# Batched attention with memory and a two-layer gated network on one core: first-layer operands of all batches split from the attention's sums, without x in DRAM

## The chip, the cores and the metric

The kernel runs on one core of a Trainium2 chip. The metric is the device time of one execution in microseconds; the time given is the median of the runs. A profiled execution has a time of its own, which is given beside its span (first to last instruction).

## The reference

Two parts run one after the other. The attention: 4 batches, 8 heads, 576 positions, 64 wide; causal softmax attention, mixed by a gate per head with a retrieval from a memory matrix. The result x, 2304 tokens by 512, goes through a two-layer network with a sigmoid gate.

```python
scores = q @ k.T / sqrt(D)                       # causal mask, softmax -> a
local = a @ v
q_p = where(q > 0, q, exp(q) - 1) + 1
mem_out = (q_p @ M_prev) / (q_p @ z_prev + 1e-6)
x = g * mem_out + (1 - g) * local                # g = sigmoid(beta), one per head
h = x @ w_in                                     # 512 -> 2048
out = (h * sigmoid(1.702 * h)) @ w_out           # 2048 -> 512
```

## The kernel before

**Precision.** The network's weights arrive as 64-bit floats. The kernel rebuilds them as 32-bit floats (`conv_unit`, `conv_pair`) and splits each operand into a high part and a low part (`xh`, `xl` for x; `wi` and `wo` for the weights); a product is three matmuls: high x high, low weight x high, high weight x low.

**Attention.** Work goes by pairs of heads: 16 pairs, four to a batch (`pairs`, index p, c is the pair within the batch). `plan_attend` lays the steps of a pair over numbered slots from `K0[p]` on: scores, softmax on VectorE and ScalarE, scaling on GpSimd, transposes, and the products with v and the memory into one PSUM tile `po` (`pv_both`; the pool `ps_o` holds one). A pair has two such sums: queries 256 to 575 (ch 1, 320 wide) and, one slot later, queries 0 to 255 (ch 0). For batch 0 the second is done up front by `first_queries`. `xboth` (L616) copies a sum to `xf` in SBUF, on VectorE for ch 1 and on ScalarE for ch 0, and keeps the copy's name in `values["po"]`; the next group of matmuls that writes `po` waits for it. Score matmuls may be put into the same group, and then wait too.

**From x to the first layer.** The first layer goes by chunks of queries, eight in all: 256 and 320 for batch 0, 288 and 288 for the others. `xstore` (L643) stores each pair's `xf` into the DRAM tile `xd`. When a batch's four pairs are done, `plan_x` (L704) loads a chunk into `xl` and `split_x` (L241) makes `xh` (ScalarE) and the low part in place (GpSimd). `xopen` (L634) does this early for the first three pairs of a batch's first chunk, if the chunk two before is done; the fourth pair then comes straight from `xf` (`xdirect`, L622). The pool `mop` holds two chunks of `xh` and `xl`. All these DMAs, the loads of later pairs and the stores of first-layer results go through the one queue of SyncE, in order.

**First layer.** `first_moe` (L724) makes for each chunk 16 blocks of 12 matmuls into `pm`; `gate` copies `pm` to `hk` (three buffers, ScalarE and VectorE in turn) and stores `hk` to the DRAM tiles `gd`.

**The order.** `step` runs a slot's planned pieces by priority, adding up a cost for each matmul (`mm`), and then fills the slot with first-layer matmuls up to the cost in `PACE`, which depends on the slot's number: L42. If the first layer has no chunk to work on, the slot stays short. The tile framework orders each engine's instructions by these priorities and its own estimate of what is ready.

**After the attention.** The attention's pools on the right side of SBUF are closed and the space is used again by `w2a` (the first five pieces of converted w_out), `opa`, `g11a` and `stg`; a tile there waits only for the tiles that lay under it. While TensorE finishes the first layer, `conv_pair` converts w_out: ScalarE scales, VectorE puts bits together and forms sums and low parts. Then the second layer runs: 84 products of 12 matmuls 384 wide, into `acc` (L935). Its fourth product is the first to use the last two pieces of w_out.

## Time and profile before

| | us |
|---|---|
| median of 3 runs | 641.17 (640.54 to 646.22) |
| profiled execution, its own time | 648.07 |
| its span | 646.3 |
| TensorE busy in the span | 602.6 (93%) |
| VectorE busy | 414.3 (64%) |
| ScalarE busy | 363.0 (56%) |
| GpSimd busy | 183.7 (28%) |
| mean granted TensorE clock | 0.985 |

PE is TensorE's matmuls, PEld its weight loads, DVE VectorE, ACT ScalarE, POOL GpSimd, SP SyncE (SPq its queue). "Released by" is what ended a wait. Matmul ends are modelled, so a busy TensorE need not be one at its peak. PEclk is the granted clock as a share of 2.4 GHz.

### The profile page before, as it was taken

The numbers are of one execution on the slowest core, as the hardware profiler recorded it, in microseconds if no ns is written. First come the engines' busy times: TensorE is split into PE (matmuls) and PEld (weight loads), VectorE is DVE, ScalarE is ACT, GpSimd is POOL, SyncE is SP. The second block draws the span as 40 slices with busy tenths as digits, with TensorE's granted clock in tenths as the row PEclk, the third lists the DMA queues.
The fourth block names the chain that finished last, engine by engine and source line by source line (L and its number), as shares of the span: only waits on it lengthen the run. The fifth ranks groups of instructions, "written<-read, shape, count | busy, mean of one in ns | idle before, by whom it ended". The sixth has DMA issues, their size and how long they took to land.

```text
span 646.3 us, 11501 instructions
## 1 busy us (share of the span) xinstructions
PE 602.6 (93%) x4000; PEld 522.7 (81%) x4000; DVE 414.3 (64%) x1015; ACT 363.0 (56%) x836; POOL 183.7 (28%) x253
## 2 busy tenths in 40 slices
PE   3698998999979999989999999899989999999997
PEld 2458765688657787778888889899989999999996
DVE  3998866654665445544455437889496579458944
ACT  4776575544564468354554335665876764776451
POOL 3556644532456433343544112310000000000000
PEclk9988999999999999999999999899999999999999
DMA  8848642323444155243342115775745630671002
GB/s 248 297 148 261 186 158 88 129 70 129 138 134 138 52 177 167 73 153 96 123 153 83 49 66 186 231 238 173 238 145 171 186 133 15 206 212 57 25 2 73
DMA packets 59370, 90.61 MB, mean 140 GB/s; under 512 B 5680, under 2 KB 48176, under 8 KB 59312
## 3 DMA queue, kind: packets, MB, share of 16 engines
q1 hardware_dynamic: 57008, 81.49, 40.1%
q0 software_dynamic: 2304, 8.39, 4.2%
q8 instruction: 31, 0.51, 0.3%
q14 instruction: 27, 0.22, 0.1%
HBM read 63.02 MB, written 26.84 MB: 139 GB/s over the span
## 4 chain that ended last, share of the span: by engine, by line
PE 66%; DMA 12%; ACT 9%; DVE 7%; issue 3%; SPq 1%; POOL 1%; DVEq 0%; ACTq 0%; POOLq 0%
PE acc L935 23%; PE pm L125 22%; PE po L125 7%; PE pt L131 7%; PE ps L125 7%; DMA gd<-hk 3%; DMA xl<-xd 3%; DMA xd<-xf 2%; DMA g<-gd 2%; ACT a L485 2%; DMA fq<-in_vq_dram 1%; DVE g L144 1%; ACT hk L136 1%; DMA qr<-in_vq_dram 1%; DVE ps L479 1%
## 5 line engine op out<-in xcount | busy, mean ns | idle before, releaser
L125 PE MATMUL pm<-xh,wi 128*128 128x288 f32 (+2 forms) x1024 | 219.4, 307 | 11.3 <-ACT hk L136 5.9
L125 PEld LDWEIGHTS pm<-xh,wi 128*128 128x128 f32 x1024 | 168.5, 194 | 14.9 <-ACT hk L136 7.0
L935 PE MATMUL acc<-oh,wo 128*128 128x384 f32 x672 | 158.3, 337 | 0.9 <-ACT oh L136 0.7
L125 PE MATMUL pm<-xl,wi 128*128 128x288 f32 (+2 forms) x512 | 154.3, 303 | 0.0
L935 PEld LDWEIGHTS acc<-oh,wo 128*128 128x128 f32 x672 | 120.0, 188 | 2.7 <-ACT oh L136 2.7
L144 DVE TENSOR_TENSOR ol<-g,oh 128x768 fp32r<-128x768 f32 x84 | 79.2, 955 | 49.0 <-ACT oh L136 44.4
L479 DVE CUSTOM_DVE_ANT_0 ps<-ps,mask 128x256 f32<-128x256 f32 (+4 forms) x144 | 67.5, 506 | 61.6 <-PE ps L125 54.8
L488 POOL TENSOR_SCALAR a<-a,sm,g 128x512 f32<-128x512 f32 (+3 forms) x112 | 71.6, 651 | 116.4 <-DVE sm L538 100.0
L935 PE MATMUL acc<-ol,wo 128*128 128x384 f32 x336 | 99.7, 339 | 2.7 <-DVE ol L144 2.6
L125 PEld LDWEIGHTS pm<-xl,wi 128*128 128x128 f32 x512 | 98.6, 193 | 1.1 <-DVE wr L216 1.1
L485 ACT ACTIVATE a<-ps,nm 128x256 f32<-128x256 f32 (+2 forms) x112 | 59.9, 542 | 63.9 <-DVE nm L479 63.1
L136 ACT ACTIVATE oh<-g 128x768 fp32r<-128x768 f32 x84 | 70.2, 840 | 42.3 <-PE acc L935 40.9
L125 PE MATMUL ps<-kqf 128*128 128x288 f32 (+4 forms) x288 | 67.9, 480 | 4.6 <-ACT at L485 2.3
L935 PEld LDWEIGHTS acc<-ol,wo 128*128 128x128 f32 x336 | 61.5, 188 | 5.3 <-DVE ol L144 5.3
L136 ACT ACTIVATE hk<-pm 128x288 f32<-128x288 f32 (+2 forms) x85 | 34.1, 410 | 38.2 <-PE pm L125 26.8
L131 PE MATMUL pt<-ident,a 128*128 128x128 f32 x296 | 53.2, 274 | 0.0
L898 ACT ACTIVATE g<-g 128x768 f32<-128x768 f32 x48 | 40.3, 844 | 20.3 <-DMA g<-gd 17.8
L125 PEld LDWEIGHTS po<-e,vr 128*64 128x64 f32 x416 | 29.9, 137 | 20.1
L131 PE MATMUL pt<-ident,at 128*128 128x128 f32 x160 | 41.4, 285 | 4.9 <-ACT a L485 3.5
L125 PE MATMUL po<-e,vr 128*64 128x320 f32 (+3 forms) x416 | 45.4, 359 | 0.0
L144 DVE TENSOR_TENSOR g<-g,g 128x768 f32<-128x768 f32 x48 | 44.1, 953 | 1.2 <-ACT g L898 1.1
L125 PEld LDWEIGHTS ps<-kqf 64*128 64x128 f32 (+1 forms) x288 | 30.1, 189 | 17.8 <-issue 7.4
(127 smaller groups left out, 751.5 us busy)
## 6 DMA issues: line engine op xcount, KB each, us to landing
g<-gd SPq DMA_DIRECT2D x48, 384.0 KB, 3.9
gd<-hk SPq DMA_DIRECT2D x96, 144.0 KB, 2.0
wraw<-in_w_out_dram POOLq DMA_DIRECT2D x16, 512.0 KB, 4.8
wraw<-in_w_in_dram SPq DMA_DIRECT2D x16, 512.0 KB, 4.8
kqf<-in_kq_dram SPq DMA_DIRECT2D x12, 608.0 KB, 6.6
vr<-in_vq_dram SPq DMA_DIRECT2D x16, 320.0 KB, 6.0
qr<-in_vq_dram SPq DMA_DIRECT2D x12, 320.0 KB, 3.2
xd<-xf SPq DMA_DIRECT2D x10, 288.0 KB, 6.4
```

Source lines behind the costliest of these rows:

```text
L125: x = nc.tensor.matmul(out, l, r, start=start, stop=stop)
L131: nc.tensor.transpose(out, in_, idn)
L136: return nc.scalar.activation(out=dst, in_=src, func=AF.Copy, **kw)
L144: (nc.vector if eng == "V" else nc.gpsimd).tensor_tensor(out=dst, in0=a, in1=b, op=op)
L479: nc.vector.tensor_tensor_reduce(out=ps, in0=ps, in1=mk, op0=ALU.add, op1=ALU.min, scale=-0.125, scalar=1e38 if j == 0 else nm[:, j - 1:j] ...
L485: return nc.scalar.activation(out=a, in_=ps, func=AF.Exp, scale=-1.0, bias=nm, accum_out=sm)
L488: (nc.vector if eng == "V" else nc.gpsimd).tensor_scalar(out=a, in0=a, scalar1=r, scalar2=gcol, op0=ALU.mult, op1=ALU.mult)
L898: nc.scalar.activation(out=t, in_=t, func=AF.Gelu_apprx_sigmoid)
L935: nc.tensor.matmul(acc[b, j][:, :QN], W[2 * p + kk][:, WPART[i], sp, 128 * j:128 * j + 128], mv[:, kk], start=first and p + kk == 0 and sp ...
```

## The change

Every sum of the attention is split straight from PSUM into `xh` (ScalarE) and `xl` (VectorE) by the new `split_sum`; `values["po"]` names the subtract. The copies to `xf`, the DRAM tiles `xd`, their stores and loads, and `split_x`, `split_direct`, `xdirect`, `xopen`, `xstore` and `plan_x` are gone. The operands of two batches are held: those of odd batches in `mop`, those of even ones in a new pool `mox`, the first on the right side. Chunks are 256 and 320 wide for every batch, and a chunk can be used from the slot after its last sum. `PACE` is 2.2 below slot 60 and 2.8 after it.

```diff
@@ -35,11 +35,10 @@
 def tile_attention_memory_moe(ctx, tc, kq, vq, mem, zz, beta, w_in, w_out, out):
     nc = tc.nc
     CH = 288
-    NCH = S // CH
     MB = 1
     KEEP = 1
     STEP = 7
-    PACE = ((20, 2.2), (60, 2.2), (9999, 2.7))
+    PACE = ((60, 2.2), (9999, 2.8))
     LATE = 4
     W0 = 6
     CONV = [-7, -6, -5, -3, -1, 1, 3, 5, 7, 9]
...
@@ -58,6 +57,7 @@
     fst = pool(first, "fst", side="left")
     ps_m = pool(left, "ps_m", 2, space=PSUM, side="left")
     dr = pool(ctx, "dr", space=bass.MemoryType.DRAM)
+    mox = pool(attn, "mox", 2, side="right")
     ldp = pool(attn, "ldp", side="right")
     att = pool(attn, "att", side="right")
     wkp = pool(attn, "wkp", side="right")
...
@@ -66,7 +66,6 @@
     ps_x = pool(attn, "ps_x", 1, space=PSUM, side="right")
     ps_o = pool(attn, "ps_o", 1, space=PSUM, side="right")
 
-    xd = [dr.tile([128, NK, S], F32, name=f"xd{b}") for b in range(B)]
     gd = [dr.tile([2, 128, NT], F32, name=f"gd{k}") for k in range(NB // 2)]
 
     moe_ps = [(ps_m, "pm")]
...
@@ -227,30 +226,24 @@
             at(slot + k, prio, fn)
 
 
-    chunks = [(b, 0, 256) for b in range(MB)] + [(b, 256, 320) for b in range(MB)]
-    chunks += [(b, CH * ch, CH) for b in range(MB, B) for ch in range(NCH)]
+
+
+    chunks = [(b, a, n) for b in range(B) for a, n in ((0, 256), (256, 320))]
     XW = max(n for _, _, n in chunks)
     xq = {}
     xplan = {}
 
     def new_x(n):
-        xl = mop.tile([128, NK, XW], F32R, name="xl")
-        xq[n] = [None, xl]
-        return xl
-
-    def split_x(n, upto=NK):
-        w, xl = chunks[n][2], xq[n][1]
-        xh = xq[n][0] = mop.tile([128, NK, XW], F32R, name="xh")
-        for c in range(upto):
-            copy("A", xh[:, c, :w], f32(xl[:, c, :w]))
-            sub("P", xl[:, c, :w], f32(xl[:, c, :w]), xh[:, c, :w])
-
-    def split_direct(n, c, src):
+        assert n < 4 or n - 4 in done, n
+        p = mop if chunks[n][0] % 2 else mox
+        xq[n] = [p.tile([128, NK, XW], F32R, name=x) for x in ("xh", "xl")]
+
+    def split_sum(n, c, src):
         w, (xh, xl) = chunks[n][2], xq[n]
         copy("A", xh[:, c, :w], src)
-        sub("V", xl[:, c, :w], src, xh[:, c, :w])
-
-    direct, done = set(), set()
+        return tt("V", xl[:, c, :w], src, f32(xh[:, c, :w]), ALU.subtract)
+
+    done = set()
 
     def first_queries(b):
         K, fsm = [], []
...
@@ -339,7 +332,7 @@
                     nc.tensor.transpose(pt[:, o:o + 128], q[:, c, t], ident)
             copy("A", qt[:, 2 * k:2 * k + 2].rearrange("p c q -> p (c q)"), pt)
 
-        def values(c, xl):
+        def values(c):
             po = (ps_o if c % 2 == 0 else ps_m).tile([128, 512], F32, name="pm" if c % 2 else "po")
             rr = [slice(64 * h, 64 * h + 64) for h in range(2)]
             for k, (l, o, mv) in enumerate((
...
@@ -348,13 +341,11 @@
                     (v[:, c, 1], 128, lambda h: fa[c][:, 512 + 128 * h:640 + 128 * h]))):
                 for h in range(2):
                     nc.tensor.matmul(po[rr[h], o:256], l[:, rr[h]], mv(h), start=k == 0, stop=k == 2)
-            copy("A", xq[b][0][:, c, :256], po[:, :256])
-            sub("V", xl[:, c, :256], po[:, :256], xq[b][0][:, c, :256])
+            split_sum(0, c, po[:, :256])
 
         if b == 0:
             gates()
-        xl = new_x(b)
-        xq[b][0] = mop.tile([128, NK, XW], F32R, name="xh")
+        new_x(b)
         score(0)
         phi()
         score(1)
...
@@ -614,40 +604,12 @@
                     mm(po[r, x:y], l[:, r], mv, first and k == 0, last and k == len(ops) - 1)
 
         def xboth(ch):
-            q0, n = (0, 256) if ch == 0 else (256, 320)
-            if ch:
-                P["xf"] = wkp.tile([128, S], F32, name="xf")
-            values["po"] = copy("AV"[ch], P["xf"][:, q0:q0 + n], U["po", ch][:, :n]).ins.name
-
-        def xdirect():
-            n = 2 * b + 1 if rest else 2 * b
-            if rest and c == 0:
-                direct.add(n)
+            n = 2 * b + ch
+            if n not in xq:
                 new_x(n)
-                xq[n][0] = mop.tile([128, NK, XW], F32R, name="xh")
-            if n in direct and (rest or c == NP - 1):
-                a, w = chunks[n][1:]
-                split_direct(n, c, P["xf"][:, a:a + w])
-                if c == NP - 1:
-                    xplan[n] = state["slot"] + 1
-
-        def xopen():
-            n = 2 * b
-            if n in direct or n - 2 not in done:
-                return
-            direct.add(n)
-            a, w = chunks[n][1:]
-            nc.sync.dma_start(f32(new_x(n)[:, :NP - 1, :w]), xd[b][:, :NP - 1, a:a + w])
-            at(state["slot"] + 2, 45, lambda: split_x(n, NP - 1))
-
-        def xstore():
-            if not rest:
-                a = CH if c == NP - 1 and 2 * b in direct else 0
-                nc.sync.dma_start(xd[b][:, c, a:], P["xf"][:, a:])
-            del prep[p]
-            raws.pop(p)
+            values["po"] = split_sum(n, c, U["po", ch][:, :chunks[n][2]]).ins.name
             if c == NP - 1:
-                xready[b] = state["slot"]
+                xplan[n] = state["slot"] + 1
 
         at(k0, 10, s_tail)
         at(k0 + 1, 10, max_tail)
...
@@ -694,22 +656,7 @@
                 at(k + 1, 12, lambda js=js: hand_on(js, pv_both, [U["ev", hh, jj] for hh in range(2) for jj in js]))
                 at(k + 1, 30, flush)
                 at(k + 1, 32, lambda ch=int(j > 0): xboth(ch))
-        if c == NP - 1 and not rest:
-            for j in range(k0 + 7, k0 + 11):
-                at(j, 5, xopen)
-        at(k + 2, 33, xdirect)
-        at(k + 2, 60, xstore)
-
-
-    def plan_x(n, slot):
-        b, a, w = chunks[n]
-
-        def load():
-            nc.sync.dma_start(f32(new_x(n)[:, :, :w]), xd[b][:, :, a:a + w])
-
-        at(slot + 1, 5, load)
-        at(slot + 2, 45, lambda: split_x(n))
-        return slot + 3
+
 
     def gate(ps, n, blk):
         b, a0, w = chunks[n]
...
@@ -724,13 +671,6 @@
     def first_moe():
         after = 0
         for n, (b, _, w) in enumerate(chunks):
-            if n not in xplan:
-                while b not in xready:
-                    yield 1
-                if n not in xplan:
-                    xplan[n] = plan_x(n, state["slot"])
-            if n >= 2 * MB and n % 2 == 0:
-                xplan[n + 1] = plan_x(n + 1, state["slot"] + (n not in direct))
             for blk in range(NB):
                 while blk not in wb or n not in xplan or state["slot"] < xplan[n]:
                     yield 1
```

## Rows read from the trace of the kernel before

**Rows 1.** The page: engines (busy us, share, instructions) and the chain that ended last, by engine and line.

```profile
PE 602.6 (93%) x4000; PEld 522.7 (81%) x4000; DVE 414.3 (64%) x1015; ACT 363.0 (56%) x836; POOL 183.7 (28%) x253
...
PE acc L935 23%; PE pm L125 22%; PE po L125 7%; PE pt L131 7%; PE ps L125 7%; DMA gd<-hk 3%; DMA xl<-xd 3%; DMA xd<-xf 2%; DMA g<-gd 2%; ACT a L485 2%; DMA fq<-in_vq_dram 1%; DVE g L144 1%; ACT hk L136 1%; DMA qr<-in_vq_dram 1%; DVE ps L479 1%
```

**Rows 2.** Busy time by stretches: length; PE, PEld, DVE, ACT, POOL; clock; DMA share; GB/s.

```profile
184.00:193.00 9.00, 5.55 (x35) 3.47 (x34) 5.34 (x22) 5.99 (x20) 4.01 (x6) 1.00 0.66 222
...
193.00:213.00 20.00, 16.89 (x110) 12.44 (x111) 9.32 (x35) 10.75 (x34) 13.62 (x18) 0.91 0.37 116
...
276.00:289.00 13.00, 10.52 (x75) 9.13 (x74) 5.33 (x19) 6.78 (x25) 4.98 (x9) 0.99 0.50 159
...
288.00:293.00 5.00, 4.71 (x25) 4.70 (x26) 0.32 (x2) 2.70 (x8) 3.19 (x5) 0.66 0.25 87
...
414.00:419.00 5.00, 4.44 (x22) 4.44 (x23) 5.00 (x11) 2.71 (x7) 2.02 (x3) 0.66 0.82 233
...
293.00:388.00 95.00, 95.00 (x732) 79.44 (x732) 46.22 (x162) 41.68 (x128) 31.96 (x43) 1.00 0.31 95
...
388.00:459.00 71.00, 68.02 (x505) 67.25 (x500) 58.38 (x105) 44.82 (x93) 14.16 (x20) 0.98 0.65 203
```

**Rows 3.** Timeline of TensorE: start, length, line, tile, count; in brackets idle before, releaser.

```profile
288.29 0.56 PE L125 MATMUL pm<-xh,wi 128*128 128x288 f32 x2 [2.44 <-ACT hk L136]
...
414.56 0.55 PE L125 MATMUL pm<-xh,wi 128*128 128x288 f32 x2 [2.01 <-ACT hk L136]
```

**Rows 4.** Timeline of SyncE's queue, the same columns, issue of DMAs.

```profile
276.37 0.33 SPq L646 DMA_DIRECT2D xd<-xf  x1
...
282.92 0.38 SPq L640 DMA_DIRECT2D xl<-xd  x1
...
283.39 11.73 SPq L720 DMA_DIRECT2D gd<-hk  x6
...
403.40 0.53 SPq L708 DMA_DIRECT2D xl<-xd  x1
```

**Rows 5.** Timeline of ScalarE, the two splits of loaded x.

```profile
286.83 1.11 ACT L136 ACTIVATE xh<-xl 128x288 fp32r<-128x288 f32 x3 [6.17 <-DMA xl<-xd]
...
410.36 1.45 ACT L136 ACTIVATE xh<-xl 128x288 fp32r<-128x288 f32 x4 [3.15 <-DMA xl<-xd]
```

**Rows 6.** Groups by line and shape: busy us, mean ns; last row one tile's view (min/median/max).

```profile
L139 DVE COPY xf<-po 128x320 f32<-128x320 f32 x16 | 7.8, 491 | 6.5 <-PE po L125 6.5
...
L136 ACT ACTIVATE xf<-po 128x256 f32<-128x256 f32 x12 | 4.5, 376 | 1.0 <-PE po L125 1.0
...
L136 ACT ACTIVATE xh<-xl 128x288 fp32r<-128x288 f32 x22 | 8.1, 432 | 16.0 <-DMA xl<-xd 16.0
...
L144 POOL TENSOR_TENSOR xl<-xl,xh 128x288 fp32r<-128x288 f32 x22 | 18.5, 869 | 21.9 <-ACT xh L136 21.9
...
L136 ACT ACTIVATE xh<-xf 128x320 fp32r<-128x320 f32 x4 | 1.8, 457 | 1.1 <-DVE xf L139 1.1
...
L144 DVE TENSOR_TENSOR xl<-xf,xh 128x320 fp32r<-128x320 f32 x4 | 2.2, 545 | 2.3 <-ACT xh L136 2.3
...
L144 DVE TENSOR_TENSOR xl<-po,xh x2: 415/418/420, 31.5 to 36.3; 128x256 fp32r<-128x256 f32 x2
```

**Rows 7.** Timelines around `po`: first a filled stretch, then one without fill.

```profile
366.43 2.22 PE L125 MATMUL po<-e,vr 128*64 128x320 f32 x20
...
371.00 0.92 PE L125 MATMUL ps<-kqf 64*128 64x256 f32 x8
...
180.41 0.49 DVE L139 COPY xf<-po 128x320 f32<-128x320 f32 x1 [0.48 <-PE po L125]
...
181.05 0.92 PE L125 MATMUL ps<-kqf 64*128 64x256 f32 x8
```

**Rows 8.** Timeline of VectorE, the last piece of converted w_out.

```profile
459.55 1.23 DVE L144 TENSOR_TENSOR wo<-st,wo 128x1024 fp32r<-128x1024 f32 x1 [2.76 <-ACT wo L136]
```

**Rows 9.** Waits of ScalarE: us in total, times, longest.

```profile
ACT hk L136 <- DMA gd<-hk: 7.7, 6, 2.3
```

More of the change, by code (lines that the diff above doesn't have):

```diff
@@ L366, in first_queries @@
         qtr(1)
[L367 removed]
+        values(0)
         score(3)
         norm(2)
[L370 removed]
+        values(1)
         norm(3)
[L372 to L373 removed]
+        values(2)
+        values(3)
     pairs = [(b, c) for b in range(B) for c in range(NP)]
```

7 lines of the change are left out of this document (1 added, 6 removed).

## The prediction

> **What bounds the kernel now.** I read the page's engine table and its chain first. TensorE is busy 602.6 of 646.3 us, so 43.7 us of idle time is all there is to win besides clock; on the chain that ended last, DMA holds 12%, with the load of x (xl<-xd) 3% and its store (xd<-xf) 2% [rows 1]. So the second question is where TensorE stands idle. The table by stretches answers it [rows 2]: from 293 to 388 us TensorE has no idle time at all, but it idles 9.00-5.55=3.45 us in 184 to 193, 20.00-16.89=3.11 us in 193 to 213 and 13.00-10.52=2.48 us in 276 to 289. Each of these stands where a batch's x has just been summed and first-layer work on it is about to begin. The timeline of TensorE names the two longest stops after that, 2.44 us at 288.29 and 2.01 us at 414.56, both released by ScalarE's copy `hk` [rows 3]; and after each the granted clock is 0.66 over 5 us [rows 2], so about 3.4 of the 5 us run at the 1.2 GHz level and the rest at 2.4 GHz: 5.00x(1-0.66)=1.7 us of work lost each time. In 193 to 213 the clock is 0.91: 20.00x0.09=1.8 us.
>
> Why would TensorE wait for an `hk` copy? SyncE's timeline and ScalarE's show it [rows 4, 5]. At 276.37 SyncE issues the store of batch 2's last sums; the load of the same data behind it may go only when that store has landed, and goes at 282.92; six `hk` stores queue behind it. ScalarE has `xh<-xl` next in its own order and stands 6.17 us, till 286.83, for the load. Behind that stands `hk`, behind `hk` the PSUM bank that TensorE needs. At 403.40 it is the same with the last chunk: its load waits for chunk 5's buffer, ScalarE stands 3.15 us and goes on at 410.36. So a store, a load and two in-order queues, and not TensorE, end the wait at batch boundaries.
>
> **The change part by part.** The sum starts from the profiled execution: 646.3 us span and 1.8 us around it, 648.07 us. The median of the three runs is 641.17 us; I subtract the same number of microseconds from it. Their scatter (640.54 to 646.22) makes about 1% what can be told from no change.
>
> *x no longer goes through DRAM.* The stores of 12 pairs, the loads of 6 chunks, their waits and the 22 + 22 splits from `xl` (ScalarE 432 ns, GpSimd 869 ns) go [rows 6]. At 184 to 213 the idle time is 6.56 us; from about 184.5, when the sum of pair 7 is split, first-layer matmuls can fill it, and I leave 1.5 us to the start of the stretch: -5.0, and -1.8 for the clock. At 276 to 289: -2.48 and -1.7. At 414: -2.01 and -1.7. Together -14.7 us. Bounds: -16.2 if nothing stays idle, and -8.5 if the idle time of the last two places remains with one of the clock's dips, from another cause (14.7-2.5-2.0-1.7).
>
> *The splits move onto the PSUM sum.* Per whole pair, before: one VectorE copy (491 ns) and one ScalarE copy (376 ns) out of PSUM, then the splits elsewhere. After: ScalarE `xh` and VectorE `xl` for both halves, about 457+376 ns and 545+418 ns by the nearest rows [rows 6]. VectorE's share rises by 0.47 us a pair; it is busy 46.22 of 95 us in 293 to 388 [rows 2], so that is hidden. What is not plainly hidden is the bank `po`, of which there is one: `values["po"]` now names the VectorE subtract, which comes after ScalarE's copy, and the next group (8 score matmuls and the 12 of the second half) stands behind it. In a filled stretch the first half ends at 368.65 and the group begins at 371.00, with first-layer matmuls between: 2.35 us of cover against 0.46+0.55+ about 0.2 of handing over =1.2 us: 0. Without fill, the copy takes 180.41 to 180.90 and the group starts at 181.05 [rows 7]: there TensorE is 0.5 us late, two such pairs: +1.0. Bounds: 0, and +4 if ScalarE's exponentials delay each of 12 pairs so that TensorE stops 0.33 us.
>
> *On the queues.* SyncE loses those 18 issues and the waits in them; the `hk` stores, and the loads of later pairs, stand behind nothing of x. GpSimd loses 22x0.87=19 us and ScalarE the 16.0 us that it stood for loads [rows 6], none of it TensorE's work: 0.
>
> *Chunks of 256 and 320 for 288 and 288.* The same 192 matmuls and columns a chunk pair: 0. Twelve matmuls of 256 columns end 1/9 sooner, so `hk` copies come faster; ScalarE stood 7.7 us for `hk` stores in the whole run [rows 9]. Only batch 3's first half runs without attention between: 0 to +2, I take 0, since those waits cost TensorE little already.
>
> *PACE 2.8 from slot 60 on (2.7 before).* It moves work and adds none: from slot 67, where batch 1 is summed, to 132 66 slots x 0.1=6.6 us of first-layer matmuls run before the attention's end instead of after. The fill must not run dry: by the planner's own costs a whole pair has some 12.1 us of attention, so 8 slots leave 8x2.8-12.1=10.3 us; four pairs use 41 of the 51 us that a batch gives (192x(256+320)/2400 plus 384x0.013). It doesn't.
>
> *What this uncovers: the conversion of w_out.* It runs after the attention, 388 to 459, where VectorE is already busy 58.38 of 71 us; its last piece starts at 459.55 [rows 2, 8] and is needed by the fourth product of the second layer, some 6 us after that layer begins (3 products of (646.3-459)/84=2.2 us). Before, TensorE is busy 68.02 us here, 1.7 of them lost to the clock, and idle 3. After, 66.3 us less 6.6 us moved: about 60 us, while the conversion needs at least its 58 us, and its first two weights now wait for the pool `mox` under them, till chunk 5 is done (403.40 before, 15 us into this stretch [rows 4]; about 8 us into it now). Lower bound 0, upper bound +7 (the conversion as late as before, 72 us from the attention's end, against 60+6): I take +2, nearer the row of VectorE's work than that of its present end, because ScalarE's standing for x (3.15 us [rows 5]) held the conversion up too.
>
> *Room.* `mox` adds 4x5 KB a partition on the right and drops `xf`; no instruction follows: 0.
>
> Sum: -14.7+1.0+0+0+2.0=-11.7 us: 636.4 us for a profiled execution, **629.5 us** against the median.
>
> From the store's issue at 276.37 to the end of ScalarE's wait for the load the rows show 10.5 us, 6.5 of them before the load may go [rows 4, 5]. The Trainium skill (DMA: Bandwidth & Descriptors, Anatomy of one DMA) gives a transfer a fixed cost of about 2 us, most of it the receipt of the write, and lets the rest grow with the bytes. The trace does not agree in this stage; by the skill's figure, an estimate, the two transfers would take some 5 us, the boundary at 276 would have cost nothing, and the sum would be -7.5 us, 633.7 us.
>
> **The rivals.**
> 1. *The conversion becomes the bound.* For it: VectorE's 82% there, and the wait for `mox`. Against: 6 us of slack at the fourth product. At its upper bound, +7, with a clock dip of 1.7: -14.7+1+7+1.7=-5.0, 636.2 us.
> 2. *The stalls only move.* If the filling matmuls are used up before the next batch is summed, the stretch of 184 to 193 comes back before batches 2 and 3: 2x(3.45+1.8)=10.5 us given back, 640.0 us. Against it stands the reserve of 10 of 51 us; for it that the planner's costs are not times.
> 3. *The bank `po` is held too long: slower.* ScalarE then VectorE empty the one bank one after the other, and ScalarE may be in the exponentials. It costs nothing until the subtract ends 2.35 us after the first half's last matmul; each microsecond beyond costs 12 us over 12 pairs. To be over 1% slower it must end (11.7+6.4)/12=1.5 us later still; at 4 us, 12x1.65=19.8 us, 649.3 us. Against: in 293 to 388 ScalarE is busy 41.68 of 95 us. The Trainium skill (VectorE: DVE Perf Modes, Rules for kernel authors) says to copy a matmul's output to SBUF first where several operations follow, which is what the change stops doing. By the rows the subtract itself isn't slower for it: 418 ns for 256 columns from PSUM, 545 ns for 320 from SBUF.
> 4. *The boundary at 276 costs less outside a profile.* The profiled execution is 648.07-641.17=6.9 us longer than the median; if the waits of [rows 4] are part of that, its 2.5+1.7 us are not there to be won: 641.17-(11.7-4.2)=633.7 us. Against: the 6.9 us may lie anywhere.
>
> **How the numbers follow.** Forecast 0.52, rival 1 0.17, rival 2 0.13, rival 3 0.10, rival 4 0.08. The likeliest case alone reaches from 625 (nothing idle left, 0 for po and conversion: -16.2) to 635 (-8.5 and +2). The range of 624 to 642 takes in rivals 1, 2 and 4; beyond it I leave rival 3 and some of rival 2 above (0.14) and 0.06 below. Faster by over 1% (under 634.8): 0.9 of the forecast, 0.35 of rival 1, 0.1 of rival 2, 0.6 of rival 4: 0.59. Slower by over 1% (over 647.6): rival 3 and a little of rival 2, 0.12. Within 1%: 0.29.
>
> **What would show it.** No xd rows and no `xh<-xl` wait on DMA in ScalarE's list; TensorE full from the first matmul of chunk 2 to the end of the attention, and clock 1.00 at the places that answer to 193, 288 and 414 (step 1). First-layer matmuls between any two pairs after batch 1 (step PACE; their lack is rival 2). Less than 2.35 us from the end of the first half to the subtract's end (po; TensorE idle at the score group, released by VectorE, is rival 3). The second layer beginning about 60 us after the last attention product, with at most 2 us of idle time in its first products for `wo` (conversion; more is rival 1). The prediction is wrong at its root if the three places are quiet and the time is still above 636: then TensorE's idle time was not what set the end.

## The result: slower by 1.25%

| us | before | after |
|---|---|---|
| median of four runs | 643.47 (640.54 to 646.22) | 653.08 (650.54 to 655.16) |
| ratio, 95% interval | | 1.0125 (1.0086 to 1.0163) |
| profiled execution, its span | 646.3 | 653.1 |
| attention's last product (`po`) begins | 388.4 | 388.0 |
| first layer's last matmul | 458.4 | 449.6 |
| last piece of w_out (`wo`) begins on VectorE | 459.6 | 466.6 |
| second layer, first matmul to end of span | 187.8 | 203.3 |

629.5 us and a range of 624 to 642 had been forecast. The table shows where to look: the first layer ends 8.8 us sooner, as meant, and the second layer takes 15.5 us longer. -8.8+15.5 is, to rounding, the 6.8 us between the spans. The medians differ by 9.6 us: the profiled execution of the kernel before was 4.6 us longer than its median and that of the changed one 2.1 us, so 2.5 us of the difference are in no trace.

The page of the changed kernel, engines and chain (by engine, then by line), beside [rows 1]: TensorE's busy time is the same. On the chain that ended last the loads and stores of x are gone, and VectorE stands at 11% (7% before).

```profile
PE 603.1 (92%) x4000; PEld 524.9 (80%) x4000; DVE 417.1 (64%) x1024; ACT 355.2 (54%) x817; POOL 164.0 (25%) x231
...
PE 64%; DVE 11%; DMA 10%; ACT 9%; issue 4%; POOL 1%; SPq 1%; DVEq 0%; ACTq 0%; POOLq 0%
PE pm L124 26%; PE acc L875 14%; PE po L124 8%; PE ps L124 8%; PE pt L130 7%; DMA g<-gd 7%; DVE ol L143 3%; ACT oh L135 2%; ACT g L838 2%; DVE g L143 1%; DMA gd<-hk 1%; DVE ps L469 1%; ACT a L475 1%; ACT at L475 1%; DMA fq<-in_vq_dram 1%
```

Busy time by stretches of the changed kernel, in the columns and mostly the stretches of [rows 2]:

```profile
184.00:193.00 9.00, 8.30 (x60) 5.79 (x58) 7.26 (x29) 6.26 (x21) 6.41 (x9) 1.00 0.45 158
193.00:213.00 20.00, 18.76 (x143) 14.13 (x142) 13.32 (x50) 12.68 (x39) 9.92 (x13) 1.00 0.29 99
276.00:289.00 13.00, 13.00 (x94) 12.02 (x93) 5.72 (x21) 6.30 (x21) 4.29 (x7) 1.00 0.35 128
288.00:293.00 5.00, 5.00 (x39) 3.22 (x37) 2.52 (x8) 1.62 (x5) 0.08 (x1) 1.00 0.09 33
414.00:419.00 5.00, 5.00 (x44) 5.00 (x44) 3.88 (x7) 3.20 (x6) 0.00 (x0) 1.00 0.40 139
293.00:388.00 95.00, 92.78 (x720) 78.43 (x716) 45.63 (x160) 44.00 (x127) 29.55 (x41) 1.00 0.30 99
388.00:450.00 62.00, 62.00 (x451) 61.84 (x447) 45.78 (x82) 31.59 (x67) 6.35 (x12) 0.97 0.59 197
450.00:480.00 30.00, 15.69 (x71) 15.05 (x69) 22.50 (x34) 22.77 (x35) 0.00 (x0) 0.77 0.54 180
```

The places that the prediction named are quiet: 8.30 of 9 us for 5.55, 18.76 of 20 for 16.89, both places behind it full, and clock 1.00 where it was 0.91 and 0.66. The last row is the loss: in the 30 us behind the first layer TensorE stands 14.3 us and its clock is 0.77. By the rows for `acc` on the two pages TensorE is idle 15.7 us in the second layer where it was 3.6, so 12.1 of the 15.5 us are idle time; two dips of the clock, 0.66 over 453 to 458 and 0.91 over 470 to 490, lose 1.7 and 1.8 us more. The timeline of TensorE, whose two rows of [rows 3] are gone, has these stops in their stead:

```profile
386.93 0.65 PE L124 MATMUL po<-qpt,ms 128*64 128x256 f32 x4 [2.06 <-DVE xl L143]
...
453.08 0.86 PE L875 MATMUL acc<-oh,wo 128*128 128x384 f32 x2 [2.60 <-ACT hk L135]
...
470.30 2.93 PE L875 MATMUL acc<-oh,wo 128*128 128x384 f32 x8 [11.72 <-ACT oh L135]
```

The long one, 11.72 us, ends when ScalarE has made the operand `oh` of the third product. Why ScalarE is late with it, its own timeline tells:

```profile
448.61 0.85 ACT L838 ACTIVATE g<-g 128x768 f32<-128x768 f32 x1 [4.39 <-DMA g<-gd]
...
465.54 1.04 ACT L135 ACTIVATE wo<-st 128x1024 fp32r<-128x1024 f32 x1
466.49 0.83 ACT L135 ACTIVATE oh<-g 128x768 fp32r<-128x768 f32 x1
467.22 2.29 ACT L838 ACTIVATE g<-g 128x768 f32<-128x768 f32 x3
469.42 1.56 ACT L135 ACTIVATE oh<-g 128x768 fp32r<-128x768 f32 x2
```

And VectorE's, where the last row answers [rows 8], 7 us later:

```profile
402.50 1.21 DVE L143 TENSOR_TENSOR wo<-r,wo 128x256 fp32r<-128x256 f32 x2 [8.01 <-ACT wo L135]
...
450.47 0.70 DVE L796 TENSOR_SCALAR ws<-ws 128x512 int32<-128x512 int32 x1 [2.72 <-ACT ws L791]
...
466.62 1.23 DVE L143 TENSOR_TENSOR wo<-st,wo 128x1024 fp32r<-128x1024 f32 x1 [1.58 <-ACT wo L135]
```

The `oh` that ends the stop is the first of the two at 469.42, ready at 470.25. The one at 466.49, right behind the high part of the last piece of w_out, and three gelus (`g<-g`) of the second layer stand ahead of it in ScalarE's order; the last low part on VectorE ends at 467.85 meanwhile. So the second layer goes on only behind the conversion's end (what ties the third product to it, `a_opc` shows below), and between the attention's end and that piece VectorE stands idle for ScalarE again and again, 20.2 us in all where it was 12.5.

In the kernel before the same product has a wait too, a short one. One row of its TensorE timeline and two of ScalarE's, not shown ahead, are

```profile
463.52 0.96 PE L935 MATMUL acc<-oh,wo 128*128 128x384 f32 x4 [0.67 <-ACT oh L136]
...
461.89 0.85 ACT L898 ACTIVATE g<-g 128x768 f32<-128x768 f32 x1 [1.77 <-DMA g<-gd]
462.64 0.83 ACT L136 ACTIVATE oh<-g 128x768 fp32r<-128x768 f32 x1
```

It is not the conversion that ends this wait: the last low part of w_out ends at 460.78 (459.55+1.23, [rows 8]), and `oh` stands behind a gelu whose load was there only at 461.9. But the conversion ended only about 1 us ahead of that load. The prediction read TensorE's stops down to 2 us and passed over this row, which shows how little slack the third product had.

### The profile page after: what moved, and what is told of

Same layout as the page of the kernel before. It is cut to its first block, busy times and chain, and to the rows that moved or that the text cites. A ratio compares the mean times of both kernels' runs of the same rounds, so it can differ in the third digit from the quotient of the medians.

```text
span 653.1 us, 11384 instructions
## 1 busy us (share of the span) xinstructions
PE 603.1 (92%) x4000; PEld 524.9 (80%) x4000; DVE 417.1 (64%) x1024; ACT 355.2 (54%) x817; POOL 164.0 (25%) x231
## 4 chain that ended last, share of the span: by engine, by line
PE 64%; DVE 11%; DMA 10%; ACT 9%; issue 4%; POOL 1%; SPq 1%; DVEq 0%; ACTq 0%; POOLq 0%
PE pm L124 26%; PE acc L875 14%; PE po L124 8%; PE ps L124 8%; PE pt L130 7%; DMA g<-gd 7%; DVE ol L143 3%; ACT oh L135 2%; ACT g L838 2%; DVE g L143 1%; DMA gd<-hk 1%; DVE ps L469 1%; ACT a L475 1%; ACT at L475 1%; DMA fq<-in_vq_dram 1%
## 5 line engine op out<-in xcount | busy, mean ns | idle before, releaser
L124 PE MATMUL pm<-xh,wi 128*128 128x320 f32 (+1 forms) x1024 | 216.9, 304 | 5.1 <-ACT hk L135 1.8
L875 PE MATMUL acc<-oh,wo 128*128 128x384 f32 x672 | 161.3, 342 | 15.3 <-ACT oh L135 12.3
L124 PEld LDWEIGHTS pm<-xh,wi 128*128 128x128 f32 x1024 | 165.8, 191 | 9.3 <-ACT hk L135 2.9
L124 PE MATMUL pm<-xl,wi 128*128 128x256 f32 (+1 forms) x512 | 153.2, 301 | 0.2 <-DVE xl L143 0.2
L875 PEld LDWEIGHTS acc<-oh,wo 128*128 128x128 f32 x672 | 122.0, 191 | 18.3 <-ACT oh L135 15.3
L478 POOL TENSOR_SCALAR a<-a,sm,g 128x512 f32<-128x512 f32 (+3 forms) x112 | 70.2, 640 | 133.6 <-DVE sm L528 120.2
L135 ACT ACTIVATE hk<-pm 128x320 f32<-128x320 f32 (+1 forms) x82 | 32.8, 412 | 52.4 <-PE pm L124 31.4
L135 ACT ACTIVATE e<-pt 128x320 f32<-128x320 f32 (+2 forms) x76 | 32.9, 438 | 23.2 <-PE pt L130 19.9
```

The source lines that it names most:

```text
L124: x = nc.tensor.matmul(out, l, r, start=start, stop=stop)
L135: return nc.scalar.activation(out=dst, in_=src, func=AF.Copy, **kw)
L478: (nc.vector if eng == "V" else nc.gpsimd).tensor_scalar(out=a, in0=a, scalar1=r, scalar2=gcol, op0=ALU.mult, op1=ALU.mult)
L875: nc.tensor.matmul(acc[b, j][:, :QN], W[2 * p + kk][:, WPART[i], sp, 128 * j:128 * j + 128], mv[:, kk], start=first and p + kk == 0 and sp ...
```

## The experiments

Twenty traces in one table, the two above among them. "Idle" is VectorE's idle time between the attention's last product and its last `wo`, worked out from the busy time by stretches; "rest" is from that last `wo` to the end of the span; "second" is from the second layer's first matmul to the end. The edits of names with b_ are made to the kernel before, those with a_ to the changed one.

| kernel | ratio to before (95%) | attention ends | last `wo` | idle | first layer ends | second | rest |
|---|---|---|---|---|---|---|---|
| before | | 388.4 | 459.6 | 12.5 | 458.4 | 187.8 | 186.7 |
| after | 1.0125 (1.0086 to 1.0163) | 388.0 | 466.6 | 20.2 | 449.6 | 203.3 | 186.5 |
| `b_p28` | 1.0164 (1.0123 to 1.0204) | 394.7 | 473.1 | 19.9 | 457.0 | 199.2 | 183.2 |
| `b_p28_k2` | 1.0138 (1.0109 to 1.0168) | 393.2 | 469.1 | 16.3 | 458.1 | 195.2 | 184.3 |
| `b_pool` | 1.0123 (1.0089 to 1.0156) | 384.2 | 455.2 | 10.6 | 458.4 | 194.4 | 197.7 |
| `b_p28_pool` | 1.0082 (1.0052 to 1.0111) | 393.9 | 466.4 | 15.1 | 456.3 | 191.9 | 181.9 |
| `b_late133_pool` | 1.0108 (1.0066 to 1.0150) | 383.7 | 452.8 | 10.0 | 460.7 | 187.7 | 195.8 |
| `a_rev` | 1.0109 (1.0079 to 1.0140) | 387.2 | 464.4 | 19.0 | 448.0 | 203.3 | 187.0 |
| `a_late24` | 0.9998 (0.9973 to 1.0023) | 390.4 | 451.0 | 3.8 | 452.7 | 189.7 | 191.5 |
| `a_rev_late24` | 1.0011 (0.9992 to 1.0030) | 390.2 | 451.8 | 4.7 | 453.0 | 188.2 | 189.5 |
| `a_late133` | 1.0011 (0.9987 to 1.0035) | 386.9 | 458.8 | 13.3 | 447.8 | 196.2 | 185.3 |
| `a_k2` | 1.0070 (1.0045 to 1.0095) | 386.6 | 462.2 | 17.4 | 450.1 | 197.8 | 185.8 |
| `a_rev_g_k2` | 1.0067 (1.0041 to 1.0093) | 385.1 | 462.2 | 17.6 | 449.4 | 198.1 | 185.5 |
| `a_opc` | 1.0074 (1.0043 to 1.0105) | 387.1 | 466.4 | 20.1 | 448.4 | 201.0 | 183.1 |
| `a_pool` | 0.9915 (0.9882 to 0.9948) | 386.4 | 456.9 | 14.6 | 448.1 | 190.4 | 181.7 |
| `a_pool_2` (same code) | 0.9941 (0.9915 to 0.9968) | 387.5 | 458.3 | 15.1 | 448.6 | 191.5 | 181.9 |
| `a_late133_pool` | 0.9998 (0.9967 to 1.0029) | 387.0 | 455.7 | 7.7 | 448.2 | 192.3 | 185.0 |
| `a_rev_g_late133_pool` | 0.9974 (0.9951 to 0.9998) | 384.7 | 457.2 | 13.1 | 449.8 | 192.7 | 185.4 |
| `a_rev_g_pool` | 0.9966 (0.9937 to 0.9995) | 384.1 | 456.2 | 13.7 | 445.2 | 194.6 | 183.7 |
| `a_opc_pool` | 0.9997 (0.9965 to 1.0029) | 390.0 | 462.1 | 15.0 | 451.7 | 194.5 | 184.2 |

Read the last column first. In every kernel whose last `wo` lies behind the first layer's end, "rest" is 181.7 to 187.0 us, whatever the first layer did. In the four whose last `wo` lies ahead of it (`a_late24`, `a_rev_late24`, `b_pool`, `b_late133_pool`) it is 189.5 to 197.7, and there "second" is 187.7 to 189.7 but for `b_pool`. So the later of the two sets the end (`b_pool`, with a stop of its own, fits neither), and in the changed kernel it is the conversion by 17 us. In the kernel before the two lie 1 us apart, and the conversion held up next to nothing yet: its "second" of 187.8 us is that of `b_late133_pool` (187.7), whose last `wo` began 7.9 us ahead of the first layer's end.

VectorE's work in between, last `wo` less attention's end less idle, is 56.8 to 59.6 us in all kernels that leave all of it on VectorE (before 58.7, after 58.4, `a_late24` 56.8): what varies is the idle time, 3.8 to 20.2 us. With it goes, in most rows, what ScalarE has in its order ahead of the last pieces. Between the attention's end and the last `wo` it runs 2 gelus of the second layer in the kernel before, 10 in the changed one, 8 in `b_p28`, 7 in `a_late133` and 1 in `a_late24`, and it stands 0, 6.6, 1.5, 2.2 and 0 us there for the loads of `g` that they need. That this order makes VectorE idle is argued from the rows; no run changes it alone.

### Is it wo0's wait for the pool under it, or the place of the conversion in the order?

`a_rev` takes the first wait away: the pieces that are converted early get pools of their own, the other way round, so that wo4 lies over `mox`.

```diff
-    w2a = pool(ctx, "w2a", side="right", reuse_waits="tile")
+    w2a = {kk: pool(ctx, f"w2a{kk}", side="right", reuse_waits="tile") for kk in reversed(range(EARLY))}
-            at(s0 + 4, 40, lambda: new_w(w2a, kk))
+            at(s0 + 4, 40, lambda: new_w(w2a[kk], kk))
```

> The changed kernel with one thing different: the pieces of w_out converted early (wo0 to wo4, pool w2a) have pools of their own, opened in reverse, so that wo4 and not wo0 lies over mox. Theory C (the end of the conversion sets the end; its first pieces were held by mox): VectorE's idle time of 8.0 us ahead of its first wo (394 to 402 us) goes, the last wo ends near 460 instead of 467.85, the second layer stops for under 4 us instead of 11.7, and the time falls by 6 to 8 us, ratio to the kernel before about 1.000. Theory P (the time is lost to TensorE's lower clock and to the slower start, the conversion only looks late): under 2 us, ratio 1.010 or more.

`a_late24` changes PACE alone, and `a_rev_late24` does both.

```diff
-    PACE = ((60, 2.2), (9999, 2.8))
+    PACE = ((60, 2.2), (106, 2.8), (9999, 2.4))
```

> The changed kernel with PACE 2.4 instead of 2.8 from slot 106 on (after batch 3's first pair has been summed, where fewer fills no longer break the planner): about 10 us of first-layer matmuls move from before the attention's end to after it. Theory C: the attention ends 8 to 12 us sooner, but wo0 still waits for chunk 5 and its mox, which ends where it did within 2 us because as many matmuls lie before it, so the conversion's end and the time stay: within 3 us of the changed kernel. Theory A (the time goes with the end of the attention alone): 8 to 12 us less. Theory W (fills moved out of the attention only cost the same later): within 1 us, and the second layer begins no sooner either.

> Both edits together: reversed pools for wo0 to wo4, and PACE 2.4 from slot 106. Theory C: attention ends about 10 us sooner and the conversion follows it, last wo near 450, ratio about 0.98 to 0.985 (636 us where the changed kernel has 653). If the two edits only add what each gives alone under Theory W, it is a_rev within 1 us.

Measured: 651.53, 643.78 and 645.44 us, the kernel before beside them 644.27. In `a_rev` the wait of 8.01 us is gone; VectorE's timeline has its first and its last `wo` at

```profile
392.69 0.42 DVE L143 TENSOR_TENSOR wo<-r,wo 128x256 fp32r<-128x256 f32 x1
...
464.41 1.23 DVE L143 TENSOR_TENSOR wo<-st,wo 128x1024 fp32r<-128x1024 f32 x1 [1.59 <-ACT wo L135]
```

The first is 9.8 us sooner, the last 2.2 us, and the idle time 19.0 us instead of 20.2: the longest wait of VectorE in this stretch was nearly free. VectorE then waited most of that time later, in other places. That part of Theory C falls. The number is the one that Theory P gave (1.0109), but not its mechanism, as the next run shows: the end still follows the last `wo` by 187.0 us.

`a_late24` gave 9 us where Theory C had said none; that is Theory A's number. But the attention did not end sooner, as Theories C and A had assumed (390.4 for 388.0, with a stop of TensorE of 3.68 us at 386.09; 444 first-layer matmuls lie behind its last product in both). What changed is the conversion: 60.6 us from the attention's end instead of 78.6, idle time 3.8.

```profile
451.04 1.22 DVE L143 TENSOR_TENSOR wo<-st,wo 128x1024 fp32r<-128x1024 f32 x1 [0.26 <-ACT wo L135]
```

It ends with the first layer, and the second layer runs 189.7 us. `a_rev_late24` has nothing left to win there: 1.0011, where Theory C had said 0.98 to 0.985.

### PACE alone, in the kernel before

```diff
-    PACE = ((20, 2.2), (60, 2.2), (9999, 2.7))
+    PACE = ((20, 2.2), (60, 2.2), (9999, 2.8))
```

> The kernel before with PACE 2.8 instead of 2.7 from slot 60 on, nothing else. It moves first-layer matmuls ahead of the attention's end and adds none. Theory C: the attention ends 3 to 7 us later, the conversion with it, and the time is 3 to 7 us longer (ratio 1.005 to 1.011). As the prediction had it (moving work costs nothing): within 1 us.

Measured: 654.85 us, ratio 1.0164, the largest loss of all runs, from one digit, and more than either expectation. The attention ends 6.3 us later and the first layer 1.4 us sooner; the last `wo` begins 13.5 us later, 6.3 of it by the later end of the attention and 7.4 by VectorE's idle time. TensorE's timeline has two stops:

```profile
464.16 1.01 PE L935 MATMUL acc<-oh,wo 128*128 128x384 f32 x2 [6.39 <-ACT hk L136]
...
476.03 1.65 PE L935 MATMUL acc<-oh,wo 128*128 128x384 f32 x4 [5.39 <-ACT oh L136]
```

and VectorE's has the last piece at

```profile
473.08 1.23 DVE L144 TENSOR_TENSOR wo<-st,wo 128x1024 fp32r<-128x1024 f32 x1 [2.48 <-ACT wo L136]
```

These are stops before the same products as in the changed kernel, without any change of x. So PACE 2.8 brings them, and against the kernel before with that same PACE the change of x is not shown to be slower or faster: 1.0125 for 1.0164, with intervals that overlap. The changed kernel with the old PACE of 2.7 was not run.

### Before or after the attention's end: where PACE acts

`a_k2` begins a piece of the conversion in every second slot after the attention instead of two in five; `a_late133` leaves 2.8 up to the attention's last slot and lowers it behind; `b_p28_k2` is `b_p28` with the denser pieces; `a_rev_g_k2` has the pools of `a_rev`, and `opa` and `g11a` opened ahead of them.

```diff
-        if (k % 5 in (2, 4) or fill["gen"] is None) and conv_q:
+        if (k % 2 == 0 or fill["gen"] is None) and conv_q:
```

for `a_k2`, `b_p28_k2` and `a_rev_g_k2`,

```diff
-    PACE = ((60, 2.2), (9999, 2.8))
+    PACE = ((60, 2.2), (133, 2.8), (9999, 2.4))
```

for `a_late133`, and for `a_rev_g_k2`, beside the lines of `a_rev`,

```diff
+    opa = pool(ctx, "opa", side="right", reuse_waits="tile")
+    g11a = pool(ctx, "g11a", 2, side="right", reuse_waits="tile")
     w2a = {kk: pool(ctx, f"w2a{kk}", side="right", reuse_waits="tile") for kk in reversed(range(EARLY))}
-    opa = pool(ctx, "opa", side="right", reuse_waits="tile")
-    g11a = pool(ctx, "g11a", 2, side="right", reuse_waits="tile")
```

> The changed kernel with one thing different: after the attention a piece of w_out's conversion is begun in every second slot instead of two in five, so that all eight are begun by the 16th slot and not by the 19th. PACE is untouched. Theory S (the conversion is planned by slots; a slot of 2.8 gives the first layer's matmuls away faster than 2.7, so they are used up before the conversion's slots are, and VectorE stands idle for ScalarE's pieces that come late in its order): the attention's last product stays near 388, VectorE's idle time between there and its last wo falls from about 18 us to under 6, the last wo ends near 452, the second layer begins near 450 without a stop over 3 us, ratio to the kernel before 0.990 to 1.000. Theory F (PACE acts through the fills that lie before the attention's end, as in the run with 2.4 from slot 106): ratio 1.010 to 1.015, as the changed kernel.

> The changed kernel with PACE 2.4 from slot 133 on, after the last slot of the attention; up to there 2.8 as in the changed kernel. Theory S: as the run with 2.4 from slot 106, ratio 0.997 to 1.004, last wo 61 to 64 us behind the attention's last product instead of 79.6. Theory F: nothing changes, ratio 1.010 to 1.015.

> The kernel before with PACE 2.8 instead of 2.7 from slot 60 on, which alone cost 1.6%, and with the conversion's pieces begun in every second slot. Theory S: the attention still ends near 395, 6.5 us later than with 2.7, but the conversion takes about 62 us from there instead of 79, ends with the first layer near 457, and the ratio is 0.998 to 1.005: moving matmuls ahead of the attention's end costs nothing by itself. If the later end of the attention is the cost: 1.010 to 1.016.

> The changed kernel with the pieces begun in every second slot, the pools of wo0 to wo4 opened in reverse, and opa and g11a opened first, so that these lie over mox and the gelu with its table load can't run before the attention's end. Theory S with the stop at 387 as a cost of its own: the stop of 2.06 us at 386.93 and the clock of 0.91 behind it go, 2 to 4 us less than with every second slot alone, ratio 0.985 to 0.995. If the stop costs nothing (the conversion or the first layer takes it up): within 1 us of every second slot alone.

Measured: 1.0070, 1.0011, 1.0138, 1.0067. `a_late133` changes no slot ahead of the attention's end and gains 1.1%, so Theory F falls: in the changed kernel it is the slots behind that count. Theory S had its ratio right, but the conversion took 71.9 us from the attention's end and not 61 to 64. A slot there holds PACE's worth of first-layer matmuls, and the conversion's pieces are planned by slots; with 2.8 the matmuls are used up in fewer slots, and ScalarE's share of the last pieces comes behind the first layer, among the second layer's gelus (the count is above). But the simple form of Theory S falls too: denser pieces brought the last `wo` to 462.2 and not to 452, and idle time to 17.4, not under 6; in the kernel before they brought 0.3%, not 1.3%, and 1.0138 lies in the range of the rival there, that the later end of the attention is the cost. ScalarE's real order is made by the framework out of plan and estimates, and denser slots alone don't mend it. `a_rev_g_k2` ends the attention 1.5 us sooner than `a_k2` and is no faster, as the second expectation had it: its conversion takes that much longer, and the last `wo` begins at 462.2 in both.

### Work taken off VectorE

Seven low parts of 128x1024, 1.22 us each on VectorE, go to GpSimd, which is idle there. `a_late133_pool` and `b_late133_pool` add PACE 2.4 from slot 133 on, `a_rev_g_late133_pool` also the pools of `a_rev_g_k2`.

```diff
-            sub("V", lo, src, hi)
+            sub("P" if len(w.shape) == 4 and w.shape[1] == 4 and kk < KK - 1 else "V", lo, src, hi)
```

> The changed kernel with the largest low part of every piece of w_out but the last (128x1024, 1.22 us of VectorE, seven of them) on GpSimd, which is idle there. Nothing else is moved. Theory V (the conversion sets the end because VectorE has too much to do in it): the last wo ends 6 to 8 us sooner, near 460, ratio to the kernel before 1.000 to 1.004. Theory O (it sets the end because ScalarE's pieces come late in ScalarE's order, and VectorE stands idle for them, 20 us between the attention's end and the last wo): VectorE's idle time grows by what its work falls, the last wo ends within 3 us of 466.6, ratio 1.008 to 1.014.

> The same with PACE 2.4 from slot 133 on, which alone gave 1.001 with the last wo at 458.8 and a first layer that ended at 447.9. Theory V: the conversion ends near the first layer, the second layer begins at 448 and runs 188 us, ratio 0.985 to 0.992. Theory O: the last wo within 3 us of 458.8, ratio 0.997 to 1.003.

> The kernel before with both of these edits. There the first layer ends at 458.5 and the last wo began at 459.6, so the first layer bounds the gain whatever the conversion does: theories V and O both say 0 to 3 us, ratio 0.995 to 1.000. The difference between this kernel and the changed kernel with the same edits is what the change of x gives once the conversion is out of its way; the first layer's end says 8 to 10 us, ratio 1.5% apart, under V.

> The changed kernel with both edits, and with opa, g11a and then wo4 to wo0 laid from mox on, so that neither the early gelu with its table load nor wo0's wait for mox remains. If the conversion is out of the way, the stop at 387 and the clock behind it come off the time: 2 to 4 us less than the two edits alone. If the conversion still sets the end: within 1 us of them.

> The changed kernel with the seven low parts on GpSimd, as in a_pool, again: 0.988 to 0.995.

Measured: 0.9915 and, again, 0.9941, both intervals under 1: faster than both kernels, by 12 to 13 us than the changed one. 0.9998, 1.0108 and 0.9974 for the other three. Both theories missed `a_pool` (1.000 at the least): the last `wo` comes 9.7 us sooner, more than the 6 to 8 of Theory V, and by another way. `a_late133_pool` has Theory O's ratio; the other two lie outside what was expected. Of the 9.7 us, 1.6 are the earlier end of the attention, 5.6 are idle time (20.2 to 14.6), and 2.5 are VectorE's own work, where seven times 1.22 us is 8.5: some of what was taken off came back. Another 4.8 us are won behind the last `wo` (186.5 to 181.7). The timeline of TensorE in `a_pool` shows what is left of the stops:

```profile
451.88 1.01 PE L875 MATMUL acc<-oh,wo 128*128 128x384 f32 x2 [2.95 <-ACT hk L135]
...
459.08 1.70 PE L875 MATMUL acc<-oh,wo 128*128 128x384 f32 x8 [1.93 <-ACT oh L135]
```

Where some of VectorE's work came back, one row of its timeline shows,

```profile
446.62 2.85 DVE L143 TENSOR_TENSOR wo<-r,wo 128x512 fp32r<-128x512 f32 x1
```

beside one of GpSimd's:

```profile
446.16 2.77 POOL L143 TENSOR_TENSOR wo<-st,wo 128x1024 fp32r<-128x1024 f32 x1 [6.75 <-ACT wo L135]
```

The stop before the third product is 1.93 us instead of 11.72. A low part of 128x512 that takes VectorE 0.69 us elsewhere took 2.85 us while GpSimd was in its own (446.16 to 448.93).

The pair that the prediction of 1.5% was made for, `a_late133_pool` and `b_late133_pool`, stands 1.1% apart, but because the kernel before got slower by the edits, which no theory had: see the next part. And VectorE's work was not always less: last `wo` less attention's end less idle is 61.0 us in `a_late133_pool` (58.6 in `a_late133`) and 60.4 in `b_pool` (58.7 before). A row of VectorE's timeline of `b_pool`, beside one of GpSimd's, is an example of why:

```profile
412.49 3.00 DVE L144 TENSOR_TENSOR st<-r,r 128x256 f32<-128x256 f32 x1
...
412.83 2.37 POOL L144 TENSOR_TENSOR wo<-st,wo 128x1024 fp32r<-128x1024 f32 x1
```

That step takes 0.42 us elsewhere. Six steps of VectorE in `b_pool` that run beside GpSimd's seven take 11.0 us longer in all than their like in the same trace, where 8.5 us had been moved.

### What the same edit does to the kernel before

`b_pool` is that edit alone in the kernel before, `b_p28_pool` the same with PACE 2.8, `a_rev_g_pool` the edit in the changed kernel with the pools of `a_rev_g_k2`.

> The kernel before with the seven low parts of 128x1024 on GpSimd, nothing else. Theory C (in the kernel before the first layer's end at 458.5 stands 2.3 us ahead of the conversion's and takes over as the bound): 0 to 3 us less, ratio 0.995 to 1.000, so that the changed kernel with the same edit, 0.9915, is 3 to 6 us better by its x alone. Rival (the edit helps both alike, by 10 us): ratio 0.980 to 0.985.

> The kernel before with PACE 2.8, which alone cost 1.64%, and the seven low parts on GpSimd. Theory C (moving matmuls ahead of the attention's end costs only through the conversion): last wo 8 to 10 us sooner than 473.1, first layer's end at 457 as before, ratio 1.000 to 1.006. If the later end of the attention costs by itself: 1.010 or more.

> The changed kernel with the seven low parts on GpSimd, and with opa, g11a, then wo4 to wo0 laid from mox on. Theory L (the early gelu's stop at 387 with its clock, and wo0's wait, cost 2 to 4 us where the conversion isn't the bound): ratio 0.985 to 0.989, against 0.9915 without. If the conversion still sets the end and starts no sooner by it: 0.990 to 0.994.

Measured: 1.0123, 1.0082, 0.9966. `b_pool` fell outside both expectations. TensorE's timeline:

```profile
413.66 0.85 PE L125 MATMUL pm<-xh,wi 128*128 128x288 f32 x2 [5.25 <-ACT hk L136]
...
464.05 1.01 PE L935 MATMUL acc<-oh,wo 128*128 128x384 f32 x2 [4.87 <-ACT hk L136]
```

and ScalarE's:

```profile
408.71 1.44 ACT L136 ACTIVATE xh<-xl 128x288 fp32r<-128x288 f32 x4 [5.69 <-DMA xl<-xd]
```

The attention ends 4.2 us sooner, but the load of the last chunk of x is there only 1.6 us sooner (408.71, and 410.36 in [rows 5]), so ScalarE stands 5.69 us for it instead of 3.15 and TensorE 5.25 instead of 2.01: the stall at 414 that the change removes takes up what other edits gain. The second stop is new: the first layer's last `hk` copies, done by 464.0 on ScalarE, stand behind a gelu of the second layer whose load was there only at 462.3, and the PSUM banks of `acc` wait for them.

At equal PACE and with this edit the pair is `b_p28_pool` and `a_pool`: 1.0082 against 0.9915 and 0.9941, 1.4 to 1.7%, or 9 to 11 us for the change of x. Without the edit the same pair is 1.0164 and 1.0125, 2.5 us. In both pairs the change of x ends the attention sooner, by 6.7 us without the edit and by 7.5 with it, and the last `wo` too, by 6.5 and 9.5. Without the edit 3.3 us of that are lost behind the last `wo` ("rest" 186.5 for 183.2), with it none. So at equal PACE the change of x brings the conversion's end forward in both pairs, and without the edit half of that does not reach the end; why is not shown. `b_p28_pool` missed its upper bound (1.006): its last `wo` came 6.7 us sooner than in `b_p28`, not 8 to 10, and still 10 us behind the first layer.

`a_rev_g_pool` ends the first layer 2.9 us sooner than `a_pool` (no stop at 387), and its second layer takes 4.2 us longer. Neither range was met. With another order of the same work the gain was given back in the second layer, where TensorE's first stop is 5.17 us for 2.95 in `a_pool`.

### Which product needs the conversion's end

The prediction had said the fourth. The third product's operand lies in the pool `opc`, over the conversion's buffers `stg`.

```diff
     pools["op", 1] = pool(ctx, "opb", side="left", reuse_waits="tile")
+    pools["op", 2] = pool(ctx, "opc", side="left", reuse_waits="tile")
...
-    pools["op", 2] = pool(ctx, "opc", side="right", reuse_waits="tile")
```

> The changed kernel with the third operand buffer opc on the left side, no longer over the conversion's buffers stg. Theory B (the third product stood for this buffer, which comes free with the last piece; the fourth needs the last piece itself): the long stop moves from the third product to the fourth, 2.2 us of matmuls go ahead of it, 1 to 3 us less, ratio 1.008 to 1.011. If ScalarE's order, in which the operand's copy stands behind the last piece of wo, holds it instead: within 1 us, ratio 1.012, the stop still ahead of the third product.

> The changed kernel with both: the seven low parts on GpSimd, and opc on the left side. If they add up: what is left of the stop before the third product (1.93 us) goes, ratio 0.986 to 0.991. If the stop of 2.95 us at the second product, where the banks of acc wait for hk copies that stand behind gelus on ScalarE, takes it up: 0.991 to 0.995.

Measured: 1.0074 and 0.9997. One row of TensorE's timeline of `a_opc`:

```profile
467.19 1.65 PE L875 MATMUL acc<-oh,wo 128*128 128x384 f32 x4 [9.71 <-ACT oh L135]
```

The view of the tile `acc` ahead of that stop (448 to 467.1; after the count, ns min/median/max, first and last start):

```profile
L875 PE MATMUL acc<-oh,wo x24: 331/335/443, 448.5 to 457.0; 128*128 128x384 f32 x24
```

The same of the changed kernel, ahead of its long stop (449 to 470.2):

```profile
L875 PE MATMUL acc<-oh,wo x16: 338/431/539, 449.8 to 458.1; 128*128 128x384 f32 x16
```

A product has eight such matmuls: 24 are three products, 16 are two. The long stop moved from the third to the fourth, as Theory B said, and "rest" fell from 186.5 to 183.1 with the last `wo` at the same time. The price of the buffer's place is one product, 0.5%, with intervals that overlap. Together with the GpSimd edit it did not add up, and 0.9997 is slower than both expectations: in the profiled execution the attention ended at 390.0, 3.6 us later than in `a_pool`, of which 2.9 are there by the first attention product (82.0 for 79.1), and the conversion took 72.1 us instead of 70.5. But that execution (648.24 us) was the slowest of twelve with a median of 642.74, so it tells little about the median. Why the first 80 us differ between kernels that are alike there was not settled.

## Why the prediction was wrong, point by point

**The three places where TensorE stood for x (-14.7): right in mechanism and nearly in size.** In 184 to 213 the idle time fell from 6.56 to 1.94 us, 4.6 where 5.0 were said; the clock came back (1.8); 2.48+1.7 at 276 to 293 and 2.01+1.7 at 414 are gone. That makes 14.3 us. (In `b_p28`, with x still loaded, PACE alone left 0.19 us of the stop at 414, at 419.06.) The wait on `po` has its two stops of 0.37 us behind unfilled pairs inside that idle time. Not foreseen: a stop of 2.06 us at 386.93 with a clock of 0.91 over 20 us behind it (1.8 us), because with the new pool on the right side `g11a` lies over other space, free before the attention's end as its loads tell: they are issued at 376.91 (450.15 before), and ScalarE, which stood 2.06 us for them, has their gelus and a table load of 1.28 us in front of the `xh` at 385.85 that empties `po`; and a start that was 2.6 us later (the first attention product at 80.6 us, 78.0 before, on a row of the tile `po`). 14.3 less these 6.5 is 7.8 of the 8.8 us by which the first layer ended sooner.

**PACE "moves work and adds none: 0": this step failed.** It does move work and add none: 492 first-layer matmuls lie behind the attention's last product before, 468 in `b_p28` (24 of 0.13 us, some 3 us) and 444 in the changed kernel. Yet it cost 10 us by itself (`b_p28`): the conversion follows the attention, which ends 6.3 us later there, and VectorE idles 7.4 us more in it; 3.5 us come back behind the last `wo`. The step asked only what TensorE does with the moved matmuls. They were the cover under which ScalarE and VectorE converted w_out, and the slots that they fill are what that conversion is planned by. The 7.4 us of idle time are the loss of the changed kernel too, whose attention ended no later than before (388.0 for 388.4): VectorE idles 7.7 us more there.

**"What this uncovers: the conversion" (+2.0, bounds 0 and +7): this step failed, in its slack and its bound.** The slack of 6 us before the fourth product was 1 to 2 us: the third product's operand waits for the last piece too (`a_opc`), and in the kernel before that operand was begun at 462.64, when the last piece had been done since 460.78. The upper bound took the conversion to be as long as before, 72 us from the attention's end; it became 79, since the same 58 us of VectorE's work met 20 us of idle time for 12.5. The trace of before had the right sum: attention's end 388.4, 71.2 to the last `wo`, 186.7 behind it. The stops ahead of the attention's end were worth 11.0 us of it (-5.0-1.8-2.48-1.7), `po` and PACE took 1.0 and 6.6 back, and what a shorter first layer saves behind it counts for nothing: 3.4 us of gain and the slack of 1 to 2, some 5 and not 11.7, before the conversion grew.

**Rival 1** (the conversion becomes the bound) was the case that came, chance 0.17, with a price of +7 where 15.5 were lost behind the first layer. Its argument was the right one and its price was held down by the false slack. **Rival 2** did not come: TensorE has no stop over 0.3 us from 200 to 380, so the fill did not run dry. **Rival 3** came once: the stop of 2.06 us at 386.93 is released by the subtract that empties `po`, which with the two stops of 0.37 us makes 2.8 us for the +1.0 of the sum; its price over 12 pairs did not come. **Rival 4** is in part answered by more runs: the kernel before has medians of 644.2 to 645.4 us over 13 to 28 of them, so of the 6.9 us between profile and median about half were the three runs that the forecast started from.

**The wait for `mox`**, the only reason that the prediction gave for a later conversion, is VectorE's longest wait in that stretch and cost 1.6 us at most (`a_rev`, whose interval overlaps that of the changed kernel).

**The root** was named at the end of the prediction: the three places quiet and the time still above 636 means that TensorE's idle time did not set the end. It did not.

What stays open: how PACE turns into ScalarE's order in detail (`a_k2` mends less than half of the loss, `a_late133` nearly all of it, by unlike ways), what the change of x gives with the old PACE, and the spread of 2 to 4 us in the first 80 us of the span.

## What to carry to other kernels

Before costing a gain on the engine with the most busy time, look for the task that ends last at the seam behind it, even where it causes no wait yet, and ask how much later it may end: write the end as a sum along that task (here attention's end + 58 us of conversion + its idle time + 186) and see which terms the change touches. Work that "only moves" is cover for something; name what ran under it, and by what it is paced. And a long wait is worth what its removal brings the last instruction of its chain: 8 us of idle time taken away at the front of the conversion came back as idle time further on.

## What the hardware showed that was not expected

VectorE's subtract of 128x512 from two operands in SBUF took 2.85 us instead of 0.69 while GpSimd ran its own subtract (446.62 to 449.47 against 446.16 to 448.93, in `a_pool`), and a step of 128x256 (`st<-r,r`) took 3.00 us instead of 0.42 (412.49 to 415.49 against 412.83 to 415.20, in `b_pool`). The Trainium skill (SBUF — State Buffer, Who interferes with whom) says that a VectorE instruction with two SBUF inputs contends with a GpSimd instruction that reads SBUF. The traces agree: the first ended 0.54 us and the second 0.29 us after GpSimd's, somewhat less than the 0.69 and 0.42 us that they take elsewhere.
